# Backward stage of an attention and feed-forward block: the query gradient's products, the filler job and the key and value sums change places inside a group of eight units

## The chip, the core and the metric

The kernel runs on one NeuronCore of a Trainium2 chip. The metric is the device time of one execution in microseconds (us). The engines work in parallel, each through its own queue in program order: PE (TensorE, matrix products into the accumulation memory PSUM), ACT (ScalarE), DVE (VectorE), POOL (GpSimd) and SP (SyncE, here only an issuer of transfers). Semaphores make one engine wait for another.

## The reference

```python
def _fwd_reference(A_x, A_wqkv, A_wo, B_x, B_w_gate, B_w_up, B_w_down):
    x = A_x                                   # 1 x 2048 x 448, bf16
    xn = _layernorm(x)
    return x + _A_ref(xn, A_wqkv, A_wo) + _B_ref(xn, B_w_gate, B_w_up, B_w_down)
# _A_ref: softmax attention, 16 heads of 28, with input and output projections
# _B_ref: (silu(x @ w_gate) * (x @ w_up)) @ w_down, 1792 hidden columns

def reference(...):
    out, vjp = jax.vjp(_f, A_x, A_wqkv, A_wo, B_w_gate, B_w_up, B_w_down)
    return (out, *vjp(grad_out))
```

The kernel returns the block's output and the gradients for the input and for five weight matrices.

## The kernel before

**First stage.** It normalizes the rows, projects queries, keys and values, runs the attention forward and, between its steps, the feed-forward part with its gradients. What the second stage needs is left in device memory.

**Second stage (lines 641 to 927), which the change is about.** It walks over 512 units. A unit is one pair of heads (8 pairs, `pr`), one chunk of 512 keys (4, `kc`) and one tile of 128 queries (16, as two windows `w` of 8, `qi`). Eight units make a group `W` (64 groups); `pos` is a unit's position in its group, 0 to 7. Heads are 28 wide and padded to 32. The order on every engine is the program's: the code writes it out by hand, no scheduler moves anything.

Each unit `k` issues in this order:
- PE: the score product of unit `k` (line 872, two products into a tile `sd`), then the ds product of unit `k-1` (line 882, two more, another `sd` tile). `sd` has three buffers of two PSUM banks.
- ACT: the exponential of the scores, `E` (line 891).
- DVE: `ds` of unit `k-1`, a product of the line 882 tile and `E` (line 899). After every second unit SP issues a DMA transposition of two units' `ds` into the group's tile `dsT` (line 901); this covers units 0 to 5 of a group.
- PE again: a fill that depends on the position.

The fills are:
- **The transposes** (`pe_transpose`, line 808): 16 on PE, for units 6 and 7 of the group before, into a third `sd` tile. ACT copies one half to `dsT`, DVE the other (line 810).
- **Key and value sums** (`acc_mm`, line 782): four products for a unit, into a PSUM tile `acc`.
- **The query gradient's products** (`dq_mm`, line 823; "dq" for short): 16 products in two halves that read the whole `dsT` of a group and write the tile `aux`. `dq_out` (lines 835, 838, 841) adds the tile to a running sum on DVE.
- **A filler job** (`job_mms`): one row block of the output (19 products, lines 746 and 748), one of the input gradient (14 products, line 752) or one column block of the projection's weight gradient (16 steps of four small products, lines 714 and 716). It writes `aux` too, in three parts of nearly the same size. `job_out` copies the result on ACT (lines 761, 725), and POOL sends it. There are jobs for groups 1 to 16, 18 to 21 and 22 to 61.

The tile `aux` has one buffer:

```python
ps_x = cst.enter_context(tc.tile_pool(name="ps_x", bufs=1, space=PSUM))
```

so a job's first product waits until the last `dq_out` has read it, and a dq's first product until `job_out` has. `dsT` has two buffers, `E` eight, `ds` five (of two units each), the job's input chunk `ck` three; `job_load(W + 2)` issues the chunk's load on SP at position 0.

Before the change the fills of group W stand like this: the last third of the job at position 1 (its first two thirds at 7 of the group before and at 0), `job_out` and the transposes at 2, sums of three units at 3, dq of group W-1 at 4 and 5, `dq_out` (ahead of that unit's `ds`) and sums of five units at 6.

**Last stage (lines 930 to 987).** It finishes the last weight gradient and the input gradient.

Of the kernel before, what the change touches and what calls it, by code (L numbers as in the profile page):

```python
# [37 lines left out]
def kernel(  # L38
# [417 lines left out]
    for fc in range(NFC):  # L456
        nxt = dW_items(fc)
        for sc in range(4):
            k = min(sc, 1)
# [196 lines left out]
    UW = 8  # L656
    units = [(pr, kc, w, qi) for pr in range(NPR) for kc in range(4) for w in range(2) for qi in range(UW)]
    N = len(units)
    NW = N // UW
# [27 lines left out]
    jobs = {i + 1: j for i, j in enumerate(order) if j}  # L687
# [49 lines left out]
    def job_mms(i, ps):  # L737
        j = jobs[i]
        if j[0] == "dwq":
            return dwq_mms(j[1], j[2], ps)  # L740
        if j[0] == "y":
            t, x = chunk[i]
            out = []
            for n in range(NFC + G):
                rhs = (wtile["wd"][:, n, :] if n < NFC else wo_pad[:, n - NFC, :D])
                out.append(lambda n=n, rhs=rhs: pe.matmul(ps[:, :D], lhsT=t[:, n, :], rhs=rhs,  # L746
                                                          start=(n == 0), stop=False))
            out.append(lambda: pe.matmul(ps[:, :D], lhsT=ident_bf[:], rhs=x[:], start=False, stop=True))
            return out
        t = chunk[i]  # L750
        w = wtile[("wg", "wu")[j[1]]]
        return [lambda n=n: pe.matmul(ps[:, :D], lhsT=t[:, n, :], rhs=w[:, n, :],  # L752
                                      start=(n == 0), stop=(n == NFC - 1)) for n in range(NFC)]
# [13 lines left out]
    E, DS, st = {}, {}, {}  # L767
# [4 lines left out]
    def acc_mm(k):  # L772
        pr, kc, w, qi = units[k]
        g, hp, qt = pr // 2, pr % 2, 8 * w + qi
        if qt == 0:
            st["acc"] = ps_acc.tile([P, 512], FP32, name="acc")
        acc, Qs, dOs = st["acc"], spt[g, 0], spt[g, 2]
        e, ds = E.pop(k), DS[k // 2][:, k % 2]
        for src, m in ((dOs, e), (Qs, ds)):
            for j in range(2):  # L780
                r = (0 if src is dOs else 64) + HP * j
                pe.matmul(acc[r:r + HP, :], lhsT=src[:, qt, 64 * hp + HP * j:64 * hp + HP * j + HP],  # L782
                          rhs=m[:, j, :], start=(qt == 0), stop=(qt == NT - 1),
                          tile_position=(0, r), skip_group_check=True)
        if qt < NT - 1:
            return
        o = outp.tile([P, 512], BF16, name="dkv_o")
        act.activation(out=o[:], in_=acc[:], func=ACT.Copy, scale=sc_col[:, 0:1])
        if kc == 0:
            dsp[pr] = (dspp.tile([P, NT, P], BF16, name="dkv_sp"),  # L790
                       dspp.tile([P, 2, 4, 2, 64], BF16, name="dq_sp"))
        kv = dsp[pr][0]

        def later():
            sp.dma_start_transpose(out=kv[:, 4 * kc:4 * kc + 4, :], in_=o[:])
            for tq, r in ((2, 0), (1, 64)):
                pool.dma_start(
                    out=dqkv_d[2 * kc:2 * kc + 2, 64 * hp:64 * hp + 64, tq * G + g, :].rearrange("k p s -> p k s"),
                    in_=o[r:r + 64, :].rearrange("p (k s) -> p k s", k=2))
        sp_later.append((k_now[0] + 3, later))  # L800

    def pe_transpose(W):

        ds, dsT = DS[W * 4 + 3], st[("dsT", W)]
        ps = ps_sd.tile([P, 2, 8, P], BF16, name="sd")
        for u in range(2):
            for i in range(8):
                pe.transpose(ps[:, u, i, :], ds[:, u, i // 4, (i % 4) * P:(i % 4 + 1) * P], ident_bf[:])  # L808
        for u, eng in enumerate((act.copy, dve.tensor_copy)):
            eng(out=dsT[:, 6 + u].rearrange("p j c q -> p (j c) q"), in_=ps[:, u])  # L810
# [16 lines left out]
    def dq_out(W):  # L827
        pr, kc, w, _ = units[W * UW]
        g, hp = pr // 2, pr % 2
        ps = st["dq"]  # L830
        if (pr, w) not in dqacc:
            dqacc[(pr, w)] = dqa.tile([P, 512], FP32, name=f"dq_acc{w}")
        acc = dqacc[(pr, w)]
        if kc == 0:
            dve.tensor_scalar(out=acc[:], in0=ps[:], scalar1=SCALE, scalar2=None, op0=ALU.mult)
            return
        if kc < 3:
            dve.scalar_tensor_tensor(out=acc[:], in0=ps[:], scalar=SCALE, in1=acc[:], op0=ALU.mult, op1=ALU.add)
            return
        o = outp.tile([P, 512], BF16, name="dq_o")  # L840
        dve.scalar_tensor_tensor(out=o[:], in0=ps[:], scalar=SCALE, in1=acc[:], op0=ALU.mult, op1=ALU.add)
        dq = dsp[pr][1]

        def later():
            sp.dma_start_transpose(out=dq[:, w].rearrange("p c s r -> p c (s r)"), in_=o[:])
            for s_ in range(2):
                k0 = 4 * w + 2 * s_
                pool.dma_start(
                    out=dqkv_d[k0:k0 + 2, 64 * hp:64 * hp + 64, g, :].rearrange("k p s -> p k s"),
                    in_=o[64 * s_:64 * s_ + 64, :].rearrange("p (k s) -> p k s", k=2))  # L850
        sp_later.append((k_now[0] + 1, later))
# [4 lines left out]
    job_load(1)  # L856
    job_load(2)
    fillers = []
    for k in range(N + UW):
        W, pos = k // UW, k % UW  # L860
        k_now[0] = k
        if k < N:
            pr, kc, w, qi = units[k]
            if pos == 0:
                job_load(W + 2)
            if pos == 4:
                extra_load(W)
            q, kv = qd[pr]
            qt = 8 * w + qi
            s_ps = ps_sd.tile([P, 2, 512], FP32, name="sd")  # L870
            for j in range(2):
                pe.matmul(s_ps[:, j, :], lhsT=q[HP * j:HP * j + HP, qt * P:(qt + 1) * P],  # L872
                          rhs=kv[HP * j:HP * j + HP, kc * 512:(kc + 1) * 512],
                          start=True, stop=True, tile_position=(HP * j, 0))
        if 1 <= k <= N:
            pr, kc, w, qi = units[k - 1]
            q, kv = qd[pr]
            qt = 8 * w + qi
            d_ps = ps_sd.tile([P, 2, 512], FP32, name="sd")
            for j in range(2):  # L880
                r = 64 + HP * j
                pe.matmul(d_ps[:, j, :], lhsT=q[r:r + HP, qt * P:(qt + 1) * P],  # L882
                          rhs=kv[r:r + HP, kc * 512:(kc + 1) * 512],
                          start=True, stop=True, tile_position=(r, 0))
        if pos == 2 and W in jobs:
            job_out(W, st["job"])
        if pos == 6 and W >= 1:
            dq_out(W - 1)
        if k < N:
            E[k] = ework.tile([P, 2, 512], BF16, name="E")  # L890
            act.activation(out=E[k][:], in_=s_ps[:], func=ACT.Exp, scale=SCALE)  # L891
        if 1 <= k <= N:
            u = k - 1
            if qi == 0:
                st[("dsT", u // UW)] = twin.tile([P, UW, 2, 4, P], BF16, name="dsT")
            if u % 2 == 0:
                DS[u // 2] = dwork.tile([P, 2, 2, 512], BF16, name="ds")
            ds = DS[u // 2]
            dve.tensor_tensor(out=ds[:, u % 2], in0=d_ps[:], in1=E[u][:], op=ALU.mult)  # L899
            if qi in (1, 3, 5):  # L900
                sp.dma_start_transpose(
                    out=st[("dsT", u // UW)][:, qi - 1:qi + 1].rearrange("p u j c q -> p (u j c) q"),
                    in_=ds[:].rearrange("p u j c -> p (u j c)"))
        while sp_later and sp_later[0][0] <= k:
            sp_later.pop(0)[1]()

        if pos == 7 and W + 1 in jobs:
            st["job"] = ps_x.tile([P, 512], FP32, name="aux")
            fillers = job_mms(W + 1, st["job"])
        if pos in (7, 0, 1):  # L910
            n = -(-len(fillers) // (3 - (pos + 1) % UW))
            for f in fillers[:n]:
                f()
            fillers = fillers[n:]
        if pos == 2 and W >= 1:
            pe_transpose(W - 1)
        if pos == 3:
            for u in range(max(k - 6, 0), k - 3):
                acc_mm(u)
        if pos in (4, 5) and W >= 1:  # L920
            dq_mm(W - 1, pos - 4)
        if pos == 6:
            for u in range(k - 6, min(k - 1, N)):
                acc_mm(u)
    while sp_later:
        sp_later.pop(0)[1]()
# [91 lines left out]
```

## Time and profile before

| | |
|---|---|
| Median of 3 runs | 1595.48 us (1595.33 to 1597.69) |
| Time of the profiled execution | 1603.39 us |
| Its span, first to last instruction | 1601.6 us |
| Mean granted clock of TensorE | 0.95 |
| Score products of the second stage (line 872) | 688.4 to 1503.6 us of the span |
| Busy: PE, DVE, ACT, POOL | 1457.0, 1128.5, 1161.7, 229.8 us |
| DVE ds (line 899), mean of 512 | 1219 ns |
| ACT exponential (line 891), mean of 512 | 1028 ns |
| Transfers of `dsT` (192): issue to landing, smallest, median, largest | 4.2, 5.5, 8.7 us |

Busy time is the sum of an engine's instructions; PE's products are pipelined, so its rows overlap and a busy PE need not run at its peak. In the groups of the profile, a row has the line, engine, operation and tile (written before the arrow, read behind it), shape, count, busy time and mean, and behind the bar the idle time before it with what ended most of it. In the waits, a row has the engine and its instruction, what it waited for, the total in us, how often and the longest. In the timeline, a row has start, duration, engine, line, tile and count, merged over neighbours of one kind. A granted clock of 1.00 is TensorE's full speed, 0.50 half of it.

### The profile page before, as it was taken

Reading aid. Unit: us, or ns where it says so; the run is one execution under the profiler, and the core shown is the slowest. Engines: PE = TensorE matmul, PEld = TensorE weight load, DVE = VectorE, ACT = ScalarE, POOL = GpSimd, SP = SyncE. Lnnn points to the kernel's source line nnn. Section 1 sums busy time; section 2 is a strip of 40 time slices with the busy share of each in tenths; the row PEclk is TensorE's granted clock in tenths of the full one; section 3 lists DMA queues with packets and bytes.
Section 4 is the critical chain, followed back from the end, with each engine's and each line's share of the span. In section 5 each row is a group of like instructions: output and inputs, shape, how many; then the busy total and the mean of one; then the engine's idle time right before and its main releaser. Section 6 shows DMA issues by size and latency. Waiting matters only on the chain.

```text
span 1601.6 us, 31404 instructions
## 1 busy us (share of the span) xinstructions
PE 1457.0 (91%) x12232; PEld 590.0 (37%) x12232; DVE 1128.5 (70%) x1489; ACT 1161.7 (73%) x1271; POOL 229.8 (14%) x434
## 2 busy tenths in 40 slices
PE   5799999999999999969889999999999899999874
PEld 3233333333333333323333344333344334433442
DVE  6465656665666665358777888888798789989535
ACT  4678888888888787637666777778787788888511
POOL 2001111111111111111010111111112111110122
PEclk7899999999999999979999999999999999999888
DMA  6556658776767669489999999999999999999852
GB/s 170 124 125 134 138 102 159 145 148 135 150 142 154 146 140 180 97 220 209 213 211 217 216 172 207 205 210 218 205 195 193 199 225 177 205 205 176 168 209 91
DMA packets 762933, 277.66 MB, mean 173 GB/s; under 512 B 729281, under 2 KB 742561, under 8 KB 762785
## 3 DMA queue, kind: packets, MB, share of 16 engines
q1 hardware_dynamic: 746800, 240.45, 77.0%
q0 software_dynamic: 14576, 34.92, 8.1%
q8 instruction: 95, 1.56, 0.4%
q10 hardware_dynamic: 1408, 0.30, 0.1%
q14 instruction: 54, 0.43, 0.1%
HBM read 64.15 MB, written 59.24 MB: 77 GB/s over the span
## 4 chain that ended last, share of the span: by engine, by line
PE 69%; DMA 10%; DVE 8%; ACT 6%; issue 4%; POOL 1%; SPq 1%; ACTq 0%; POOLq 0%; DVEq 0%
PE s_ps L613 9%; PE sd L872 8%; PE f_ps L375 8%; PE f_ps L401 7%; PE aux L752 6%; PE acc L782 5%; DMA dsT<-ds 5%; PE o_ps L590 5%; PE aux L823 4%; PE aux L746 4%; PE sd L882 4%; ACT dsT L810 3%; PE sd L808 3%; PE f_ps L181 3%; DVE dsT L810 2%
## 5 line engine op out<-in xcount | busy, mean ns | idle before, releaser
L899 DVE TENSOR_TENSOR ds<-sd,E 128x1024 bf16<-128x1024 f32 x512 | 608.3, 1219 | 88.3 <-PE sd L882 39.8
L891 ACT ACTIVATE E<-sd 128x1024 bf16<-128x1024 f32 x512 | 524.0, 1028 | 195.3 <-PE sd L882 130.8
L617 ACT ACTIVATE eT<-s_ps 128x1024 bf16<-128x1024 f32 x512 | 496.6, 1021 | 130.4 <-PE s_ps L613 127.8
L872 PE MATMUL sd<-KV,QD 32*128 32x512 bf16 x1024 | 205.4, 395 | 38.4 <-DVE dsT L810 19.1
L882 PE MATMUL sd<-KV,QD 32*128 32x512 bf16 x1024 | 206.2, 393 | 8.5 <-ACT E L891 4.3
L613 PE MATMUL s_ps<-qT,kT 32*128 32x512 bf16 x1024 | 196.8, 392 | 0.0
L782 PE MATMUL acc<-E,dOsp 128*32 128x512 bf16 x1024 | 143.4, 405 | 0.1
L782 PE MATMUL acc<-ds,Qsp 128*32 128x512 bf16 x1024 | 143.4, 405 | 0.0
L872 PEld LDWEIGHTS <-QD 32*128 32x128 bf16 x1024 | 60.9, 91 | 221.7 <-issue 212.1
L401 PE MATMUL f_ps<-xnT,wgu 128*128 128x512 bf16 x448 | 118.3, 383 | 7.5 <-DVE w_sb L427 7.5
L823 PE MATMUL aux<-dsT,Ksp 128*32 128x512 bf16 x1024 | 92.2, 411 | 24.3 <-DMA dsT<-ds 24.2
L590 PE MATMUL o_ps<-eT,v_sp 128*32 128x512 bf16 x1024 | 103.6, 397 | 6.8 <-DMA v_sp<-vT 6.8
L613 PEld LDWEIGHTS <-kT 32*128 32x128 bf16 x1024 | 47.4, 91 | 161.0 <-issue 156.9
L752 PE MATMUL aux<-W,ck 128*128 128x448 bf16 x448 | 101.6, 355 | 0.0
L882 PEld LDWEIGHTS <-QD 32*128 32x128 bf16 x1024 | 77.6, 91 | 63.9 <-issue 51.1
L375 PE MATMUL f_ps<-xn_sp,f_sp 128*128 128x448 bf16 x448 | 100.3, 357 | 0.3 <-DVE hduT L435 0.3
L375 PEld LDWEIGHTS <-f_sp 128*128 128x128 bf16 x672 | 59.3, 98 | 72.5 <-issue 22.0
L810 DVE COPY dsT<-sd 128x1024 bf16<-128x1024 bf16 x64 | 44.3, 692 | 53.1 <-ACT dsT L810 53.1
L808 PE MATMUL sd<-ident_bf,ds 128*128 128x128 bf16 x1024 | 70.4, 223 | 2.8 <-DVE ds L899 2.2
L810 ACT COPY dsT<-sd 128x1024 bf16<-128x1024 bf16 x64 | 64.9, 1014 | 11.1 <-PE sd L808 6.7
L413 DVE SCALAR_TENSOR_TENSOR g<-t_sb,f_ps 128x512 f32<-128x512 f32 x56 | 38.4, 685 | 46.0 <-ACT t_sb L411 46.0
L808 PEld LDWEIGHTS <-ds 128*128 128x128 bf16 x1024 | 60.4, 99 | 17.4 <-issue 15.3
(129 smaller groups left out, 1680.7 us busy)
## 6 DMA issues: line engine op xcount, KB each, us to landing
ck<-hO_d SPq DMA_DIRECT2D x17, 576.0 KB, 5.1
hO_d<-hduT SPq DMA_DIRECT2D x56, 128.0 KB, 3.3
da_d<-hduT SPq DMA_DIRECT2D x56, 128.0 KB, 3.0
du_d<-hduT SPq DMA_DIRECT2D x56, 128.0 KB, 3.2
ck<-da_d SPq DMA_DIRECT2D x16, 448.0 KB, 4.4
ck<-du_d SPq DMA_DIRECT2D x16, 448.0 KB, 4.0
dq_c<-dqkv_d SPq DMA_DIRECT2D x8, 768.0 KB, 4.5
dqkv_d<-dkv_o POOLq DMA_DIRECT2D x64, 64.0 KB, 3.8
```

Of the source, the lines that this page charges most:

```text
L375: pe.matmul(acc[:, :D], lhsT=src[:, t, wi, :], rhs=rhs[:, t, :D], start=(t == 0), stop=(t == NT - 1))
L401: pe.matmul(st[name][:], lhsT=w(c), rhs=src[:, tsl, c, :], start=(c == 0), stop=(c == 3))
L590: pe.matmul(o_ps[HP * hh:HP * (hh + 1), :], lhsT=v[:, kt, HP * hh:HP * (hh + 1)], rhs=e[hh // 2][:, hh % 2, :], start=(kt == 0), stop=(kt ...
L613: pe.matmul(s_ps[:, j, :], lhsT=kT[r:r + HP, kt * P:(kt + 1) * P], rhs=qT[r:r + HP, qc * 512:(qc + 1) * 512], start=True, stop=True, tile_ ...
L617: act.activation(out=e[:], in_=s_ps[:], func=ACT.Exp, scale=SCALE)
L752: return [lambda n=n: pe.matmul(ps[:, :D], lhsT=t[:, n, :], rhs=w[:, n, :], start=(n == 0), stop=(n == NFC - 1)) for n in range(NFC)]
L782: pe.matmul(acc[r:r + HP, :], lhsT=src[:, qt, 64 * hp + HP * j:64 * hp + HP * j + HP], rhs=m[:, j, :], start=(qt == 0), stop=(qt == NT - 1 ...
L810: eng(out=dsT[:, 6 + u].rearrange("p j c q -> p (j c) q"), in_=ps[:, u])
L872: pe.matmul(s_ps[:, j, :], lhsT=q[HP * j:HP * j + HP, qt * P:(qt + 1) * P], rhs=kv[HP * j:HP * j + HP, kc * 512:(kc + 1) * 512], start=Tru ...
L882: pe.matmul(d_ps[:, j, :], lhsT=q[r:r + HP, qt * P:(qt + 1) * P], rhs=kv[r:r + HP, kc * 512:(kc + 1) * 512], start=True, stop=True, tile_p ...
L891: act.activation(out=E[k][:], in_=s_ps[:], func=ACT.Exp, scale=SCALE)
L899: dve.tensor_tensor(out=ds[:, u % 2], in0=d_ps[:], in1=E[u][:], op=ALU.mult)
```

## The change

The fills change places inside the group; no instruction of the body is added or taken away, and the loop runs four positions longer, for what is left over at the end.

| position | before | after |
|---|---|---|
| 0 | job, second third | dq of group W-2, first half |
| 1 | job, last third | dq of group W-2, second half |
| 2 | `job_out`; transposes of group W-1 | transposes of group W-1 |
| 3 | sums of units 5 to 7 of group W-1 | the same; `dq_out` of group W-2 behind the unit's `ds` |
| 4 | dq of group W-1, first half | job W, first third |
| 5 | dq of group W-1, second half | job W, second third |
| 6 | `dq_out`; sums of units 0 to 4 | job W, last third |
| 7 | job of group W+1, first third | `job_out`; sums of units 0 to 4 |

```diff
-    for k in range(N + UW):
+    for k in range(N + UW + 4):
...
-        if pos == 2 and W in jobs:
+        if pos == 7 and W in jobs:
             job_out(W, st["job"])
-        if pos == 6 and W >= 1:
-            dq_out(W - 1)
         if k < N:
             E[k] = ework.tile([P, 2, 512], BF16, name="E")
             act.activation(out=E[k][:], in_=s_ps[:], func=ACT.Exp, scale=SCALE)
...
+        if pos == 3 and W >= 2:
+            dq_out(W - 2)
         while sp_later and sp_later[0][0] <= k:
             sp_later.pop(0)[1]()
 
-        if pos == 7 and W + 1 in jobs:
+        if pos in (0, 1) and W >= 2:
+            dq_mm(W - 2, pos)
+        if pos == 2 and 1 <= W <= NW:
+            pe_transpose(W - 1)
+        if pos == 3:
+            for u in range(max(k - 6, 0), min(k - 3, N)):
+                acc_mm(u)
+        if pos == 4 and W in jobs:
             st["job"] = ps_x.tile([P, 512], FP32, name="aux")
-            fillers = job_mms(W + 1, st["job"])
-        if pos in (7, 0, 1):
-            n = -(-len(fillers) // (3 - (pos + 1) % UW))
+            fillers = job_mms(W, st["job"])
+        if pos in (4, 5, 6):
+            n = -(-len(fillers) // (7 - pos))
             for f in fillers[:n]:
                 f()
             fillers = fillers[n:]
-        if pos == 2 and W >= 1:
-            pe_transpose(W - 1)
-        if pos == 3:
-            for u in range(max(k - 6, 0), k - 3):
-                acc_mm(u)
-        if pos in (4, 5) and W >= 1:
-            dq_mm(W - 1, pos - 4)
-        if pos == 6:
-            for u in range(k - 6, min(k - 1, N)):
+        if pos == 7:
+            for u in range(min(k - 7, N), min(k - 2, N)):
                 acc_mm(u)
```

## The prediction

> **What bounds the kernel now.** I read the page first, then the waits, then the timeline of one ordinary group of the backward stage and of disturbed ones.
>
> ```profile
> PE 69%; DMA 10%; DVE 8%; ACT 6%; issue 4%; POOL 1%; SPq 1%; ACTq 0%; POOLq 0%; DVEq 0%
> ...
> L823 PE MATMUL aux<-dsT,Ksp 128*32 128x512 bf16 x1024 | 92.2, 411 | 24.3 <-DMA dsT<-ds 24.2
> ```
> ```profile
> DVE dsT L810 <- ACT dsT L810: 53.1, 64, 2.0
> PE aux L823 <- DMA dsT<-ds: 24.2, 13, 3.6
> PE sd L872 <- DVE dsT L810: 19.1, 62, 0.4
> ```
>
> The chain is mostly PE. What PE waits for in the backward stage is of two kinds: 13 long waits of the query gradient's products (dq, L823) for the DMA transposition of ds, and 62 short ones of the score product for DVE's copy of PE's own transposes. That DVE copy always starts after ACT's copy of the other half (64 times). I call a unit's place in its group its position (0 to 7). Here is an ordinary group from position 2 on; the columns are start, duration, engine, line.
>
> ```profile
> 1002.08 0.39 PE L872 MATMUL sd<-KV,QD 32*128 32x512 bf16 x2
> 1002.71 1.07 PE L808 MATMUL sd<-ident_bf,ds 128*128 128x128 bf16 x16
> 1003.81 1.01 ACT L810 COPY dsT<-sd 128x1024 bf16<-128x1024 bf16 x1
> 1004.48 0.39 PE L782 MATMUL acc<-E,dOsp 128*32 128x512 bf16 x2
> 1004.86 0.69 DVE L810 COPY dsT<-sd 128x1024 bf16<-128x1024 bf16 x1 [0.75 <-ACT dsT L810]
> 1005.46 3.48 DVE L899 TENSOR_TENSOR ds<-sd,E 128x1024 bf16<-128x1024 f32 x3
> 1005.60 0.39 PE L872 MATMUL sd<-KV,QD 32*128 32x512 bf16 x2 [0.29 <-DVE dsT L810]
> 1006.12 0.61 PE L823 MATMUL aux<-dsT,Ksp 128*32 128x512 bf16 x8
> 1006.73 0.39 PE L872 MATMUL sd<-KV,QD 32*128 32x512 bf16 x2
> 1007.10 0.39 PE L882 MATMUL sd<-KV,QD 32*128 32x512 bf16 x2
> 1008.86 0.68 DVE L841 SCALAR_TENSOR_TENSOR dq_o<-aux,dq_acc 128x512 bf16<-128x512 f32 x1
> 1010.08 1.12 PE L752 MATMUL aux<-W,ck 128*128 128x448 bf16 x5
> ```
>
> Score products (L872) stand at 1002.08 and again at 1013.82: 11.74 us for the group, and nearly all groups of input-gradient rows ("dx") take 11.75. Groups with rows of the output ("y", 19 products) take 12.29, those with query/key/value weight gradients ("dwq") 11.76. After PE's transposes (1002.71) DVE is backed up: copy, then ds three times without a gap, to 1008.94; only then dq_out (L841). Before, dq_out had until 1010.08, when the job reopened the single aux bank, and PE was meanwhile busy with the long key and value sum. A disturbed group, PE alone:
>
> ```profile
> 780.57 0.39 PE L823 MATMUL aux<-dsT,Ksp 128*32 128x512 bf16 x2
> 783.95 1.04 PE L823 MATMUL aux<-dsT,Ksp 128*32 128x512 bf16 x6 [2.98 <-DMA dsT<-ds]
> ```
>
> Two products run, the others wait for the DMA until 783.95, then run at half clock (0.61 each row where 0.39 is usual).
>
> **Part 1, removed: late transpositions.** dq moves from positions 4, 5 of the next group to 0, 1 of the one after: four units later, over 5 us. The largest hole at position 4 is 4.2 us over an ordinary unit (group 42), so I take all of them as covered. What they cost is read from the groups' lengths over 12.29, 11.75 or 11.76, which takes in the half clock behind them: groups 6, 8, 9, 10, 14: 5.5+1.8+3.0+4.1+1.3; 22, 24, 25, 26: 4.2+1.3+2.6+3.5; 32: 5.1; 40, 42: 4.6+4.9; the small ones together 1.3. Sum 43 us, of which 24 are the waits of L823 in the table. Bounds 24 to 43; I take **-43**.
>
> **Part 2, added: the job waits for dq_out at position 4.** The aux bank holds in turn the job and dq. Now the order is dq at 0, 1; dq_out at 3, on DVE behind that unit's ds; job from 4. So DVE's queue after the transposes is copy, ds, dq_out, and the first job product stands behind all three. From the start of the transposes (T = 1002.71): ACT copy starts at T+1.10, DVE copy at T+2.15, the first ds at T+2.75 (1005.46), dq_out can start 1.16 later (3.48/3) less its overlap of 0.03, T+3.88, lasts 0.68, and PE follows 0.06 later: **T+4.62**. PE would be ready where dq started, 1006.12 = T+3.41. So PE stands 1.21 us. Queued behind the waiting product on PE: everything, first the score product of position 5.
>
> What the rest of the group makes of this needs three more prices from the same rows. The ds product of a unit (L882) starts no sooner than 1.51 after its score product (1005.60 to 1007.10; the exponential takes 1.02 of it, and its buffer must be free). The fill starts 0.32 after it, or 0.33 after the score product where nothing waits. Fills: five, four products of a job 1.05, 0.86; the five-unit sum 1.20; half a dq 0.55; three-unit sum as it is. From T for a dx group:
> job T+4.62, +1.05 to position 5; position 5: 0.33+1.05 = 1.38; position 6: wait 0.13 (1.51-1.38), 0.32+0.86, 1.31; position 7: wait 0.20, 0.32+1.20, 1.72; position 0: 0.33+0.55 = 0.88; position 1: wait 0.63, 0.32+0.55, 1.50; position 2 up to the transposes: wait 0.18 (ACT's two exponentials back to back), 0.32, 0.50. Sum 12.96 against 11.75: **+1.21**. So the wait is not absorbed: the short dq fills now stand side by side and wait 0.63 for the exponential, about what the old order lost at positions 2, 3, 5 and 6 (0.3 each at most). The same for y (7, 6, 6 products: 1.43, 1.24, 1.24) gives 13.60 (**+1.31**) and for dwq (1.12, 1.0, 1.0) 12.98 (**+1.22**). Groups where a job meets a dq: 2 to 61 but 17, that is 15 y, 12 dwq, 32 dx: 19.7+14.6+38.7 = **+73**. The same arithmetic on the old order gives 11.81 for 11.75 and 12.50 for 12.29, so it may be 0.1 too slow here; bounds 0.9 and 1.3 a group, +53 to +77.
>
> **Part 3, with one answer.** The ACT copy of a job's result leaves position 2, where it delayed the exponential by 0.13 us, for 7, where the long sum covers it; the transposes themselves end no sooner, so the chain above keeps its length: 0. Key and value sums at 7 instead of 6: the exponential's eighth buffer is asked for behind them on PE anyway: 0. SP: the chunk load at position 0 waits for the previous job, now done at 6 of the group before; the ds transposition queued behind it at position 2 would be a unit late at worst, 1.3 us, of its ten units of lead: 0. That transposition also waits for dq at position 1, which PE has passed by then: 0. Query gradient rows leave through SP and POOL five units later; the dwq jobs that need them start eight units behind dq_out, about 11 us against 5.5 us median landing: 0. Ends: group 1 loses its dq (-1.2) and the tail gains it (16 products, one dq_out) among waits of 0.5 to 1.35 us that are there already: -1 to +3, I take 0.
>
> **Part 4, the clock.**
>
> ```profile
> 809.50:815.00 5.50, 3.53 (x40) 1.01 (x36) 4.27 (x5) 3.80 (x5) 1.21 (x2) 1.00 0.97 221
> 823.70:827.70 4.00, 2.26 (x29) 0.70 (x24) 2.75 (x4) 1.82 (x3) 0.00 (x0) 1.00 0.86 173
> 827.70:831.10 3.40, 3.40 (x32) 0.81 (x24) 2.93 (x3) 1.92 (x2) 0.00 (x0) 0.50 0.82 221
> ```
>
> These stretches give length, busy time by engine (PE first) and then the granted clock. A hole of 1.46 us in group 8 left it at 1.00; one of 1.47 in group 9, in a stretch with PE busy 57%, halved it for 3.4 us, and position 6 then took 3.06 for 1.78: 1.28 lost. The new hole is 1.2, behind waits of 0.2 and 0.4, so about 60% busy: on the edge. Bounds 0 and 59 x 1.28 = 75; I take three groups, **+4**, as most holes of this size left the clock alone.
> [...]
>
> **Sum** against the profiled execution (1603.4; span 1601.6): -43+73+4 = +34, 1637. The median of the runs is 1595.5, 7.9 below it; the same step gives **1630**. If those 7.9 are late transfers that other runs lack, the gain is 35 and the time 1637.
>
> **Rivals.**
> 1. The clock falls often. For: the edge above. Against: holes of 1.3 and 1.5 us in groups 14 and 8 did nothing. In one group of three: 20 x 1.28 = 26 for 4, so 1652. Chance 0.19. [...] No hole of 1.2 us at each group is in this trace.
> 2. Faster: the aux wait is covered. DVE would have to reach dq_out before PE reaches the job, as when the DVE copy does not stand behind ACT's (0.69 beside 1.01 us would end about 0.7 sooner). Then only part 1 is left: 1595.5-43 = 1552. It decides at a wait of 43/59 = 0.73 us. Against: the copy stood behind ACT's 64 times of 64. Chance 0.06.
> 3. Transfers stay late: SP's queue is so full (the DMA row reads 9 of 10 all through the stage) that dq waits at position 0 as well. 43 is not gained: 1673. Against: no hole over 4.2 us. Chance 0.05.
> 4. The change doesn't part dq from its transfer by four units: ruled out by the code, 0.01.
>
> My forecast has 0.67; 0.02 is for losses and gains that cancel. Faster 0.06, same 0.02, slower 0.92 (a difference under 0.2%, 3 us, can't be told from none). The range goes from the low wait (+53, 1610) to rival 1, 1655.
>
> **What would show it.** L752, L746 and L714 idle on DVE (dq_out's line), near 1.2 us in some 59 places; no wait of L823 on the DMA; dx groups near 12.96 and y groups near 13.6 us; DVE in the order copy, ds, dq_out behind the transposes; granted clock falling in few groups. Groups of 11.8 us would prove part 2 wrong, dq waiting at position 0 part 1.

## The result and the profile after

The changed kernel takes 1675.88 us (median of 4 runs, 1669.23 to 1681.58) where the kernel before takes 1595.4. The ratio is 1.0488, 95% interval 1.0446 to 1.0530: 80 us slower, and outside the predicted range of 1610 to 1655. The profiled execution has a span of 1679.8 us, 78.2 more than before.

What PE waits for from 660 us on, with the columns as before:

```profile
PE sd L872 <- DVE dsT L810: 36.8, 62, 0.6
PE sd L808 <- DVE ds L897: 28.2, 62, 0.5
PE aux L752 <- DVE dq_acc L838: 18.2, 16, 1.1
...
PE aux L746 <- DVE dq_acc L838: 9.1, 8, 1.1
PE aux L752 <- DVE dq_o L841: 9.1, 8, 1.1
PE aux L752 <- DVE dq_acc L835: 9.1, 8, 1.1
PE aux L714 <- DVE dq_acc L838: 6.8, 6, 1.1
...
PE aux L823 <- DVE dq_o L841: 1.7, 1, 1.7
```

No row with a wait of dq (L823) for the transposition is left. In its place stand two waits in each group. The job (L752, L746, L714) waits for dq_out in 59 places of 1.14 us, 67 us in all (58 rows name a line of dq_out; the 59th, in group 10, names a load of `x_c`, but it too ends 0.05 us behind dq_out). The transposes (L808) wait for ds 62 times, 28.2 us in all. Before, that row was small:

```profile
PE sd L808 <- DVE ds L899: 2.2, 5, 0.7
```

One dx group of the changed kernel, from its second short unit on:

```profile
1040.44 0.39 PE L882 MATMUL sd<-KV,QD 32*128 32x512 bf16 x2 [0.24 <-ACT E L889]
...
1041.31 0.39 PE L872 MATMUL sd<-KV,QD 32*128 32x512 bf16 x2
...
1042.24 1.05 PE L808 MATMUL sd<-ident_bf,ds 128*128 128x128 bf16 x16 [0.49 <-DVE ds L897]
...
1044.37 0.69 DVE L810 COPY dsT<-sd 128x1024 bf16<-128x1024 bf16 x1 [1.06 <-ACT dsT L810]
...
1044.98 1.21 DVE L897 TENSOR_TENSOR ds<-sd,E 128x1024 bf16<-128x1024 f32 x1
...
1046.11 0.68 DVE L841 SCALAR_TENSOR_TENSOR dq_o<-aux,dq_acc 128x512 bf16<-128x512 f32 x1
...
1046.85 1.11 PE L752 MATMUL aux<-W,ck 128*128 128x448 bf16 x5 [1.14 <-DVE dq_o L841]
```

The order on DVE is copy, ds, dq_out, and the job's first product comes 4.61 us after the first transpose. The new wait is one line above the copies: the transposes begin 0.93 after their unit's score product (1041.31 to 1042.24).

The clock in three neighbouring stretches (length, busy time by engine with PE first, then the granted clock):

```profile
1028.50:1031.90 3.40, 1.76 (x20) 0.69 (x18) 2.38 (x4) 2.94 (x3) 0.00 (x0) 0.99 1.08 181
1031.90:1035.30 3.40, 3.31 (x12) 1.02 (x12) 1.78 (x3) 0.70 (x1) 0.00 (x0) 0.50 0.97 192
1035.30:1038.70 3.40, 3.40 (x36) 1.19 (x34) 2.64 (x3) 2.67 (x4) 0.56 (x1) 1.00 0.96 234
```

In the first stretch PE is busy for 1.76 of 3.40 us, with the job's wait at its end. In the next the clock is half, and the job's first third takes 2.0 us instead of 1.1. From group 23 on this comes at every fourth or fifth group, 54.6 or 68 us apart: 16 or 20 periods of 3.41 us, the shortest time that the clock stays at one value in these traces (3.413 us in both, before and after).

The clock's record shows why it is so regular. Every stretch at one value, except the last, which the end cuts off, is a whole multiple of 3.413 us to within 0.01 us (55 of 56 stretches; 41 of 42 in the kernel before), so all changes lie on one grid. Cut along this grid, groups 2 to 61 of the changed kernel have 227 stretches at full clock. PE's products cover 0.45 to 0.62 of each of the 16 that stand ahead of a drop. Of the other 211 only three are as low (0.55, 0.56 and 0.56); the next has 0.63.

Measured against its own parts, groups 2 to 61 without 17, in us:

| | before | after | difference |
|---|---|---|---|
| median y group (15) | 12.29 | 13.96 | 25 |
| median dwq group (12) | 11.76 | 13.32 | 19 |
| median dx group (32) | 11.75 | 13.33 | 51 |
| what single groups took over their median, summed | 42 | 22 | -20 |
| all other stretches | | | 3 |

The last row is what remains of the 78.2.

### The profile page after: what moved, and what is told of

Its sections match the earlier page's. It is cut to its first block, busy times and chain, and to the rows that moved or that the text cites. A ratio compares the mean times of both kernels' runs of the same rounds, so it can differ in the third digit from the quotient of the medians.

```text
span 1679.8 us, 31404 instructions
## 1 busy us (share of the span) xinstructions
PE 1445.6 (86%) x12232; PEld 596.7 (36%) x12232; DVE 1138.4 (68%) x1489; ACT 1161.6 (69%) x1271; POOL 229.7 (14%) x434
## 5 line engine op out<-in xcount | busy, mean ns | idle before, releaser
L897 DVE TENSOR_TENSOR ds<-sd,E 128x1024 bf16<-128x1024 f32 x512 | 617.8, 1220 | 140.1 <-PE sd L882 71.3
L752 PE MATMUL aux<-W,ck 128*128 128x448 bf16 x448 | 110.5, 379 | 36.4 <-DVE dq_acc L838 18.2
L872 PEld LDWEIGHTS <-QD 32*128 32x128 bf16 x1024 | 55.1, 91 | 235.1 <-issue 225.4
L782 PE MATMUL acc<-E,dOsp 128*32 128x512 bf16 x1024 | 138.0, 393 | 0.1
L782 PE MATMUL acc<-ds,Qsp 128*32 128x512 bf16 x1024 | 138.1, 393 | 0.0
L882 PEld LDWEIGHTS <-QD 32*128 32x128 bf16 x1024 | 77.7, 91 | 56.1 <-issue 40.7
L808 PE MATMUL sd<-ident_bf,ds 128*128 128x128 bf16 x1024 | 68.3, 220 | 28.3 <-DVE ds L897 28.2
L823 PE MATMUL aux<-dsT,Ksp 128*32 128x512 bf16 x1024 | 78.9, 387 | 1.7 <-DVE dq_o L841 1.7
L808 PEld LDWEIGHTS <-ds 128*128 128x128 bf16 x1024 | 62.9, 98 | 41.8 <-issue 41.7
L752 PEld LDWEIGHTS <-ck 128*128 128x128 bf16 x448 | 40.2, 101 | 87.4 <-issue 67.1
```

## The experiments

Each run was timed against the kernel before on the same chip; the ratio is to that kernel. All but the two lag versions and the three spread versions start from the changed kernel. Falls of the clock are counted in the second stage from group 1 on.

**dq_out ahead of the copy.** The test of the largest term.

```diff
-        if pos == 3 and W >= 2:
+        if pos == 2 and W >= 2:
             dq_out(W - 2)
```

> The changed kernel with one line moved: dq_out goes to DVE at position 2, behind that unit's ds and ahead of the copy of the transposes, where DVE stands idle for 1.06 us in each group of the changed kernel. Theory A (the job's wait for dq_out is the main loss, and this hole also makes the clock fall every fourth group): no wait of L752, L746, L714 on DVE; dx groups of 12.2 us (13.33 changed, 11.75 before), y 12.85, dwq 12.2; the wait of the transposes for ds stays at 0.4; no clock drops; time 59 x 1.15 = 68 and some 21 of clock below 1676: about 1585. Rival B (DVE is simply full behind the transposes and dq_out pushes the copy back): score product of position 4 waits 0.6 longer, groups of 12.8, about 1640. Rival C (the clock falls for the short dq units, not for the hole): groups of 12.2 but drops go on, about 1606.

Measured: 1599.70 us, ratio 1.0024 (0.9996 to 1.0052). The job's wait is gone, the clock falls 4 times in the backward stage for 17, and groups take 12.25 (dx) and 12.77 (y). So A holds for the hole and the clock, and B and C are out; but the time is 15 us over A's. In the profiled execution single groups took 12 us over their medians. PE's first, then DVE's waits:

```profile
PE sd L808 <- DVE ds L897: 27.1, 61, 0.5
PE sd L872 <- DVE ds L897: 17.1, 30, 2.2
```

```profile
DVE ds L897 <- DMA dsT<-ds: 27.8, 22, 3.1
```

The last row is new. ds waits for its own buffer, which a late transposition still reads. dq has the same lead as in the changed kernel, which has no such row at all: with groups a microsecond shorter, the transfers are late again, for another reader.

**The hole kept, but filled.**

```diff
-            for j in range(2):
+            for j in list(range(2)) * (5 if pos == 4 and W in jobs and W >= 2 else 1):
                 r = 64 + HP * j
                 pe.matmul(d_ps...
```

> The changed kernel with PE kept busy in the hole: at position 4 of each group with a job the two ds products (line 882) are issued five times over instead of once, with the same result; some 0.9 us of products that nobody needs, in the 1.14 us in which PE waits for dq_out. Theory A (the clock falls every fourth group because of this hole): the groups stay at 13.3 and 13.95 us, the drops at position 4 vanish, and the time goes down by some 20 us, to about 1655, although PE does more. Rival B (the drops come from the short units and the slower pace altogether): drops as before, 1676. Rival C (the extra products delay ds of position 4, which DVE then does later): groups longer by up to 0.9, 1700 or more.

Measured: 1656.34, ratio 1.0360 (1.0302 to 1.0419), as A said. PE's waits:

```profile
PE sd L808 <- DVE ds L897: 28.3, 63, 0.5
...
PE aux L752 <- DVE dq_acc L838: 4.4, 16, 0.3
```

Groups keep 13.33, 13.96 and 13.31 us, and what they took over that, 22 us in the changed kernel, is 0.4. In none of them does the clock fall, and PE's products cover at least 0.69 of every stretch of the clock's grid in them. So B and C are out: idle PE in this hole made the clock fall, and that cost some 20 us (1675.88 to 1656.34) beside the hole itself.

**The sums dealt out anew.** The test of the wait that the prediction had not seen.

```diff
+        if pos in (0, 1):
+            for u in range(max(k - (6, 6)[pos], 0), min(k - (5, 3)[pos], N)):
+                acc_mm(u)
...
-            for u in range(max(k - 6, 0), min(k - 3, N)):
+            for u in range(max(k - 5, 0), min(k - 3, N)):
...
-            for u in range(min(k - 7, N), min(k - 2, N)):
+            for u in range(min(k - 7, N), min(k - 5, N)):
```

> The changed kernel with the key and value sums dealt out anew: one unit at position 0, three at 1 (beside the two dq halves), two at 3, two at 7; all else as changed. Theory A (the transposes of the changed kernel wait 0.41 a group because their accumulation tile takes the buffer of the ds product of position 1, whose ds comes late behind two short units): with the units at 0 and 1 longer this wait goes to 0; the job's wait for dq_out stays at 1.1 to 1.3; dx groups 13.05, y 13.85, dwq 13.2; about 12 us below the changed kernel, 1664, if the clock falls as often. Rival B (the transposes wait for the ds of the group's last unit, which is late whatever the units at 0 and 1 do): the wait stays at 0.4 and the time at 1676 or above.

Measured: 1667.14, ratio 1.0432 (1.0403 to 1.0461). The transposes' wait falls from 28.2 us to 1.6:

```profile
PE aux L752 <- DVE dq_acc L838: 18.2, 16, 1.1
...
PE sd L808 <- DVE ds L897: 1.6, 6, 0.3
```

Theory A holds for the wait. The undisturbed dx group is 12.8 us, shorter than expected, but every second dx group now takes 14.4: the clock falls 26 times instead of 17. Two groups, 12.8 and 14.4, last 27.3 us, 8 periods of 3.41: the hole meets the clock's grid at the same point every second group. This swallowed most of the gain.

**Both edits.**

> Both edits together: dq_out ahead of the copy and the sums dealt out anew. Theory A: neither the job nor the transposes wait; dx 11.9, y 12.7, dwq 12.1; 12 us below the version with dq_out early alone, about 1573; no clock drops. Rival B (the two waits hide each other, so that together they give no more than the larger): as with dq_out early alone, about 1585.

Measured: 1591.55, ratio 0.9977 (0.9950 to 1.0003). It is 8 us below dq_out early alone, with groups of 11.88 (dx), 12.53 (y) and 11.85 (dwq) at the median, each 0.2 to 0.4 shorter; so the two waits add up and don't hide each other. The absolute time misses by 18 us, as above: ds waits 29.6 us for transpositions, and single groups took 28 us over their medians.

**A sixth ds buffer in that version.**

```diff
-    dwork = ast.enter_context(tc.tile_pool(name="dwork", bufs=5))
+    dwork = ast.enter_context(tc.tile_pool(name="dwork", bufs=6))
```

> The version with dq_out early and the sums dealt out anew, with six ds buffers instead of five (two units more before DVE must wait for the transposition that reads a buffer). That version at five buffers has groups of 11.88 us (dx) and 12.53 (y), 28 us of lengthening over that in single groups, and DVE's ds waits 29.6 us for transpositions. Theory A (the transpositions come late only in bursts, where weights and rows of the next pair load too, and two more units cover most of it): ds waits under 10 us, lengthening about 10 us, time about 1575. Rival B (the transfer queue is full for so long that any buffer fills up): waits and time as before, 1591.

Measured: 1589.16, ratio 0.9952 (0.9926 to 0.9977). In time B holds: the difference to the five-buffer version, 2 us, is within the noise. In the waits neither quite does. DVE's row is gone, and PE has one again:

```profile
PE aux L823 <- DMA dsT<-ds: 13.1, 13, 3.3
```

The lateness went on to the next reader. The waits are under half of what they were (13.1 us for 29.6), but single groups still took 23 us over their medians, for 28.

**Lead alone, in the kernel before.** Each dq keeps its place but belongs to one group earlier, with `dsT` as two half tiles in five buffers. The part of the edit that moves the lead:

```diff
-        if pos in (4, 5) and W >= 1:
-            dq_mm(W - 1, pos - 4)
+        if pos in (4, 5) and W >= 2:
+            dq_mm(W - 2, pos - 4)
...
-        if pos == 6 and W >= 1:
-            dq_out(W - 1)
+        if pos == 6 and W >= 2:
+            dq_out(W - 2)
```

> The kernel before with only the lead of the transfers lengthened: every fill keeps its place, but the dq of group W-1 at positions 4 and 5 becomes that of group W-2, eight units more lead; dsT is kept as two half tiles in five buffers, and two small tiles of the dwq jobs get one buffer instead of two, for room. Theory A (the late transpositions cost what the lengthened groups show, 43 us in the profiled execution, and nothing else hangs on them): no DMA wait of L823, all groups at 11.75 and 12.29, a few us for the tail and the first dwq job: about 1555 to 1562. Rival B (the transfer queue is the bound and the waits come back in another place, in ds for its buffer or in the chunk loads): 1580 to 1595, with DVE or the job waiting for DMA.

Measured: 1604.75, ratio 1.0045 (1.0013 to 1.0077). PE's and DVE's waits:

```profile
PE aux L717 <- DMA dq_sp<-dq_o: 15.0, 2, 8.1
```

```profile
DVE ds L900 <- DMA dsT<-ds: 27.5, 25, 2.7
```

Nothing like 43 us came of it. Two dwq jobs (groups 18 and 50) now met a query gradient still under way, which is the edit's own cost; and the transpositions were late for ds instead of dq. The next run takes the first of these away: the jobs behind the y rows come one group later.

```diff
-    order = [("y", t) for t in range(NT)] + [None] + [("dwq", 0, c) for c in range(4)]
+    order = [("y", t) for t in range(NT)] + [None, None] + [("dwq", 0, c) for c in range(4)]
```

> The kernel before with eight units more lead for the transfers, and the jobs from the first weight-gradient one on a group later, so that the two dwq jobs that met a query gradient still under way (groups 18 and 50, some 9 us longer each) find it ready. Theory A (of the 43 us of the kernel before, lead alone removes what dq waited for; what the transfer queue is late beyond that comes back as ds waiting for its buffer): 18 us below the version without this shift, 1587; ds waits for transpositions near 27 us as there. Rival B (the two long groups gave the queue time to catch up, so that removing them lengthens others): within 5 us of 1605.

Measured: 1587.83, ratio 0.9927 (0.9897 to 0.9958), as A said. DVE's ds still waits 28.7 us for transpositions. Eight units of lead, with the jobs shifted, are worth some 12 us against the kernel before; the shift without the lead was not run.

**dq behind the transposes.** From the kernel before, with dq of group W-2 and most sums put where PE otherwise waits for the copies.

```diff
-        if pos == 6 and W >= 1:
-            dq_out(W - 1)
+        if pos == 6 and W >= 2:
+            dq_out(W - 2)
...
-        if pos in (4, 5) and W >= 1:
-            dq_mm(W - 1, pos - 4)
...
+        if pos in (2, 3) and W >= 2:
+            dq_mm(W - 2, pos - 2)
+        if pos >= 2:
+            for u in {2: (7,), 3: (7,), 4: (7, 6), 5: (6,), 6: (6, 5, 4)}.get(pos, ()):
+                if 0 <= k - u < N:
+                    acc_mm(k - u)
```

> The order of the kernel before with dq of group W-2 at positions 2 and 3, behind the transposes, six units more lead than before, and the key and value sums dealt out behind it (one unit at 2 and 3, two at 4, one at 5, three at 6); job at 7, 0, 1 and dq_out at 6 as before. Theory A (what counts is that each unit's products on PE cover the 1.51 us from score product to ds product, and that PE has work while the copies of the transposes run): groups of 11.5 (dx), 11.9 (y) and 11.5 (dwq), no wait of dq for the DMA; late transpositions come back as waits of ds for its buffer, some 30 us instead of 43; about 1565. Rival B (the backward stage is bound by its transfers, and shorter groups only turn into transfer waits): groups shorter, but lengthening of 45 us or more, 1585 to 1595.

> The same with six ds buffers. Theory A: ds waits for transpositions mostly gone, about 1550. Rival B (queue full): as with five, within 5 us.

Measured: 1601.60, ratio 1.0047 (1.0021 to 1.0073), with five ds buffers, and 1599.19, 1.0017 (0.9992 to 1.0042), with six. Both fall short of A, and the sixth buffer changes no more than its rival B said. Only every second dx group reaches 11.4 us, the others 11.8; and the two dwq jobs stall here as well, groups of 22 us. With the jobs shifted as above:

> The version with dq at positions 2 and 3 and six ds buffers, and the same shift of the later jobs by one group. Theory A: the two groups lengthened by some 10 us each go to 11.8; 1579, the fastest of all. Rival B: as above, 1595 or more.

Measured: 1581.89, ratio 0.9888 (0.9853 to 0.9922), near A's 1579 and the fastest of all, below the kernel before and the changed one. ds still waits for transpositions:

```profile
DVE ds L899 <- DMA dsT<-ds: 21.9, 19, 2.9
```

By the code, the first transposition of a group has to wait here for dq at position 3, which reads the `dsT` buffer that it writes. It starts within 0.1 us behind that dq in 12, 15 and 3 of 60 groups in the three versions, in the order above, and later in the others. What this adds to the lateness was not tested.

## Why the prediction was right in direction and wrong in size

**Part 2, the job's wait for dq_out: right.** From the first transpose to the job it forecast 4.62 us and the trace has 4.61; the wait is 1.14 for a forecast 1.21, in 59 places. Moving the one line took the hole away and left the rest.

**The walk round the group: one step failed, worth 21 us.** "Position 2 up to the transposes: wait 0.18 ..., 0.32, 0.50" should have been 0.91. All other steps of the dx walk stand in the trace within 0.02 (units of 1.37, 1.32, 1.71, 0.87 and 1.50 for 1.38, 1.31, 1.72, 0.88 and 1.50). The prediction let the transposes start as soon as PE was free. But their accumulation tile is the next of three buffers in turn, the one that the ds product of position 1 was put in. That product starts 0.63 late behind two short units, and its ds 0.52 after that. So the transposes wait 0.4 us, and dx groups take 13.33 for a forecast 12.96. In each of groups 2 to 61 the transposes start 0.05 us behind the end of this ds; the ds of the last unit that they read themselves had ended at least 1.18 us before, so it isn't the cause. The working asked for a free buffer at the ds product, and not at the transposes. With longer units at 0 and 1 the wait fell to 1.6 us in all.

**Part 4, the clock: mis-sized, +4 for some 22.** The mechanism was named and its price per event was about right (groups longer by 1.5 us on average, for 1.28). How often it comes was a guess that most holes of this size do nothing; in the changed kernel the clock falls 17 times in the stage, 15 of them in such a hole. Rival 1 (one group in three, 26 us) was nearer here. The forecast counted what earlier holes had done, but those came singly. The new hole comes at a fixed place of a nearly constant period, so that it drifts along the clock's grid of 3.41 us, and at regular intervals one stretch takes in most of it with the smaller waits ahead of it (PE was busy for 1.76 of 3.40 us in the first of the three stretches shown with the result). There a gap of 1.14 us, with one of 0.60 ahead of it, was enough, and in the run with the hole filled none of groups 2 to 61 with a job had a drop.

**Part 1, the late transpositions: the number was right, the reason only half.** The changed kernel has no such wait, and the 42 us of long groups are gone. The prediction gave this to four units more lead. The same lead at 12.25 us a group left 27.8 us of waits in another place, and eight units more lead in the old order brought 12 us. So a part of the 43 was bought by the slower pace, which gives the transfer queue time to catch up; that the number came out was in part luck. The traces show it on SP. From group 2 to 61 SP's transfer rows cover 0.76 of the time in the changed kernel, 0.91 before and 0.93 with dq_out early. A transposition starts on SP 0.03 us at the median behind the ds that it reads in the changed kernel, 1.1 us before and 4.7 with dq_out early. With the hole filled and with the sums dealt out anew, which stay slow, it is 0.03 as well. Rival 2's price of 1552 rested on the same reason: with the hole covered the kernel took 1600, and with both new waits gone 1592.

**Part 3:** nothing in it turned up. Of the 3 us in all other stretches, 2.4 lie ahead of the second stage (its first score product starts at 690.7 us for 688.4), in code that the change leaves as it was.

**Sum:** 34 forecast, 78 in the profiled execution. 21 of the difference is the walk, 18 the clock, 3 the other stretches; part 1 makes up 1.

## What to carry to other kernels

When work moves inside a fixed rotation of accumulation buffers, write down for every user, the rare ones too, which earlier user its buffer had and who frees it; one user left out cost more here than all rounding together. An instruction that frees a shared bank belongs where its engine is idle anyway: one line, put ahead of a copy that had to wait, was worth 76 us of 80 here. More lead for one reader did not remove the late transfers here (24.2 us of waits of dq before, 27.5 of ds with eight units more lead): look for the next reader of the same buffers, and ask whether the queue has time to catch up.

## What the runs showed of the hardware

In the changed kernel a pause of 1.14 us at one place of each group halved TensorE's clock for 3.41 us at regular intervals: from group 23 on in every fourth or fifth group, at 13.3 us a group. In the sums run, with the same pause and groups of 12.8 us, it was every second dx group. Changes of the clock lay on a grid of 3.413 us in the traces before and after. In the changed kernel, falls came behind grid stretches in which PE's products covered 0.45 to 0.62, and three stretches of 0.55 to 0.56 had no fall behind them. No sharp limit comes out of these traces: in the sums run stretches from 0.53 to 0.65 did both, and with both edits one fall came behind 0.74. Products that nobody needs, issued into that pause, made the kernel about 20 us faster (1656.34 us for 1675.88).
